# Linear attention ahead of a mixture of experts: state summed in PSUM, copied by ScalarE, state products in four quadrants, query decays made on the chip, gating work put off

## The chip, the core and the metric

The kernel runs on one core of a Trainium2 chip. A core has TensorE (PE: matrix products into PSUM; its weight loads are shown as PEld), VectorE (DVE), ScalarE (ACT), GpSimd (POOL), SyncE (SP, which here only issues transfers) and 16 DMA engines between HBM and the on-chip memory SBUF. Each engine works through its own list in order and waits on semaphores for the others. The metric is the device time of one execution in microseconds (us).

## What is computed

```python
state = zeros(B, H, D, D)                       # 4 batches, 8 heads, 64 x 64
for t in range(S):                              # 768 tokens of a batch
    state = gamma[h] * state + outer(k[:, :, t], v[:, :, t])
    y[:, :, t] = scale * (q[:, :, t] @ state)
x = y as (3072 tokens, 512)
logits = x @ w_gate                             # 8 experts, the largest takes the token
out = gate_w * sigmoid(x @ w_output_gate)[e] * (relu(x @ w1[e]) @ w2[e])
h = out @ w_in                                  # 512 x 2048
y = (h - tanh(h)) @ w_out                       # 2048 x 512
```

## The kernel before

The attention is computed in chunks of 128 tokens: 4 batches of 6 chunks make 24 tiles, n = 0 to 23, and c = n % 6 is the chunk within its batch. A chunk needs four products per head. *Scores*, k times q of the same chunk (L351), are masked and decayed by VectorE into `pt` (L344). The *state product* (L388) takes the 64 x 64 state `st` left by the earlier chunks of the batch and `qd`, the queries times a decay that depends on c (L362, GpSimd). The *masked product* (L392) takes v and `pt` and adds to the same bank, `o`. The *state update* (L405), kd times v with 128 tokens of depth, gives `up`; VectorE copies it to the next state (c = 0, L414) or adds it to the last one (L416). Chunk 0 of a batch has no state product, chunk 5 no update. All four are float32 products, which TensorE does in two passes, so eight heads make 16 instructions. Two heads form a pair hp and share a row of tiles: the head j = 0 of a pair lies on partitions 0 to 63, j = 1 on 64 to 127. Its features take the same half as its output half, so the state product of j = 0 uses the upper left quadrant of the array and that of j = 1 the lower right.

ScalarE copies `o` to `xT` (L410). TensorE turns it to token rows and computes the gate logits in one go (`tr`, L433); ScalarE copies the rows to `xr` (L436) and sends them to HBM (`xtok`, L441), VectorE sums the logits (`lp`, L440).

The loop over n (L596) writes this order into every engine's list: load of tile n + 3 (SP, four buffers `ld`), stores that are pending, from n = 5 on four loads `m` of a later weight (L207), expert weights at n = 15, 16, 17, then `attend(n)` (the last three products), `scores(n + 2)`, the work listed in `after` (ranks and slots of a finished group) and `rows(n)`. The decays of the queries are a table in HBM of 256 KB for each c from 1 to 5, loaded behind tiles 1 to 5 (L334).

The gating is done in groups of 12, 6 and 6 tiles. At a group's last tile come `onehot` (the chosen expert, L461 to L476), `values` (the table `ohv` of what is to be summed per slot, L484, L488), `chosen` (`z`, L499), and one tile later `ranks` (each token's place with its expert: small products `pre`, `rank`, and one mark `ohr` of 432 columns per tile, L516). `scale` (gate weights, from L540) fills the rest of `ohv`. `slots` multiplies marks and values into `ip` (L576) and adds them to `idxf` (L579), from which the index lists for the gathers come after the last tile (L684). The last group is cut at 3 and 5 tiles, and its last tiles are done behind the loop, which this text calls the tail.

VectorE's work that may wait stands in the lists `scales` and `convs`; `convs` splits the weight `m` in two parts by nine steps (VectorE's are L224 to L239, ScalarE's `keep` L221). `pump` issues what stands first in a list for ScalarE or GpSimd. At the end of each turn `fill([scales, convs], MOST)` issues VectorE's, up to a cost of MOST = 2.0; steps of `convs` are booked at 0.65, others at 0.2.

```python
def fill(lists, most):
    for ops in lists:
        while ops and ops[0][0] == "V" and most > 0:
            most -= ops[0][2] if len(ops[0]) > 2 else 0.2
            ops.pop(0)[1]()
```

Of the kernel before, what the change touches and what calls it, by code (L numbers as in the profile page):

```python
# [8 lines left out]
F32 = mybir.dt.float32  # L9
# [55 lines left out]
C_K = C_Q + (NCH - 1) * NPAIR * P  # L65
# [3 lines left out]
NCONA = C_W8 + E  # L69
# [5 lines left out]
NCONB = B_BIAS + 3  # L75


def const_tables():
# [7 lines left out]
    for c in range(1, NCH):  # L86
        for h in range(H):
            col = C_Q + ((c - 1) * NPAIR + h // 2) * P
            a[(h % 2) * D:(h % 2 + 1) * D, col:col + P] = SCALE * gam[h] ** (c * P + p)[None, :]
# [12 lines left out]
    return a.astype(np.float32), b.astype(np.float32)  # L102
# [7 lines left out]
def kernel(  # L110
# [179 lines left out]
    with ExitStack() as actx:  # L290
        psa = actx.enter_context(tc.tile_pool(name="psa", bufs=2, space=PSUM))
        banks.update(po=(psa, 2), pb=(psa, 2), pu=(psa, 1), pt=(psa, 3))
# [9 lines left out]
        st = [a1p.tile([P, NPAIR, D], F32, name=f"st{i}") for i in range(2)]  # L302
# [3 lines left out]

        loaded, pts, qds, kds, xts = {}, {}, {}, {}, {}

        def load(n):
            t = ap_.tile([P, 4, DM], F32, tag="ld", name=f"ld{n}", bufs=4)  # L310
            if n == 0:
# [4 lines left out]
                nc.sync.dma_start(ca[:, C_K:C_IOTA], cona[:, C_K:C_IOTA])  # L316
                nc.sync.dma_start(t[:, 2:4], qkv[n, :, 2:4])
# [8 lines left out]
            if n == 4:  # L326
                nc.sync.dma_start(ca[:, C_IOTA:], cona[:, C_IOTA:])
# [4 lines left out]
            if 1 <= n < NCH:  # L332
                col = C_Q + (n - 1) * DM
                nc.sync.dma_start(ca[:, col:col + DM], cona[:, col:col + DM])  # L334
            loaded[n] = t

        def scores(n):
# [20 lines left out]
            if c > 0:  # L358
                qd = ap_.tile([P, DM], F32, tag="qd", name=f"qd{n}", bufs=3)
                for half in (slice(0, DM // 2), slice(DM // 2, DM)):  # L360
                    col = C_Q + (c - 1) * DM + half.start
                    nc.gpsimd.tensor_tensor(  # L362
                        out=qd[:, half], in0=t[:, 0, half], in1=ca[:, col:col + DM // 2], op=ALU.mult
                    )
                qds[n] = qd
# [12 lines left out]
        def attend(n):  # L378
# [10 lines left out]
            for hp, j, r in heads:  # L389
                vs = hp * P + j * D  # L390
                ks = (j * NPAIR + hp) * P
                nc.tensor.matmul(  # L392
                    o[r, hp * P:(hp + 1) * P],
                    t[:, 3, vs:vs + D],
                    pt[:, ks:ks + P],
                    start=(c == 0 and hp == 0),
                    stop=(hp == NPAIR - 1),
                )
            qds.pop(n, None)
            if c < NCH - 1:  # L400
                up = bank("pu", f"up{n}")
                kd = kds.pop(n)
                for hp, j, r in heads:
                    head = slice(hp * P + j * D, hp * P + (j + 1) * D)
                    nc.tensor.matmul(  # L405
                        up[r, hp * D:(hp + 1) * D], kd[:, head], t[:, 3, head], start=(hp == 0),
                        stop=(hp == NPAIR - 1),
                    )
            xT = ap_.tile([P, DM], F32, tag="xT", name=f"xT{n}")
            nc.scalar.activation(xT, o, AF.Copy)  # L410
            if c < NCH - 1:
                new, old, add = st[(n + 1) % 2].rearrange("p a e -> p (a e)"), st[n % 2], up[:, 0:NPAIR * D]
# [178 lines left out]
        load(2)  # L591
        J0 = 2 * NFM - NPA
        convs, scales, soon, after = [], [], [], []
        nconv = 0
        firsts = [sum(GROUPS[:i]) for i in range(len(GROUPS))]
        for n in range(NT - 1):  # L596
# [15 lines left out]
            if n > 0:  # L612
                attend(n)
            pump(scales, False)
# [19 lines left out]
            if g + 1 in cuts[1:]:  # L634
# [3 lines left out]
                values(*a)  # L638
                chosen(*a)
# [12 lines left out]
            fill([scales, convs], MOST)  # L652
# [549 lines left out]
```

## Time and profile before

| | us |
|---|---|
| three runs | 1028.24, 1020.76, 1024.3 |
| median | 1024.3 |
| the profiled execution, its time | 1021.1 |
| its span in the trace | 1019.2 |

Times are microseconds unless marked ns. The profile is one execution; the span is what lies between its first and last instruction. A row of PE with x16 stands for the 16 passes of one product of a tile. In brackets behind a row of a timeline is the idle time of the engine just before it and what ended it. The profile's clock column gives the granted clock of TensorE as a share of full speed, and its DMA share is the mean busy share of the 16 DMA engines.

### The profile page before, as it was taken

How to read it: one execution, taken by the hardware profiler on the slowest of the kernel's cores; microseconds unless marked ns; L12 is line 12 of the kernel's file. 1: busy time of each engine (PE TensorE's matmuls, PEld its weight loads, DVE VectorE, ACT ScalarE, POOL GpSimd, SP SyncE). 2: the span in 40 equal slices, each digit the busy share in tenths (PEclk: the TensorE clock that was granted, in tenths of full speed). 3: DMA queues.
4: the chain of work that ended last, by engine and by line, in shares of the span. 5: the costliest groups of instructions: out<-in, count | busy, mean ns of one | idle time of the engine just before them, and what ended most of it. 6: DMA issues, size and time to landing. Idle time of an engine off the chain costs nothing.

```text
span 1019.2 us, 15927 instructions
## 1 busy us (share of the span) xinstructions
PE 984.2 (97%) x5754; PEld 844.1 (83%) x5754; DVE 789.6 (77%) x1193; ACT 575.5 (56%) x1008; POOL 429.7 (42%) x359
## 2 busy tenths in 40 slices
PE   8998979999999999999999999999999999999995
PEld 6887858899999999998888888888888888888884
DVE  3588867999999999944987777777777777777772
ACT  1332314545545455545876766677676667767662
POOL 4464514375575664642333343253334325333322
PEclk9999998999999999999999999999999999999998
DMA  8997633567476576764200010010001001000001
GB/s 317 368 333 269 250 117 121 167 224 229 155 250 194 185 234 191 250 194 169 73 21 11 32 32 21 1 52 22 11 32 32 22 1 51 12 1 22 21 1 44
DMA packets 43415, 120.54 MB, mean 118 GB/s; under 512 B 9410, under 2 KB 14274, under 8 KB 40514
## 3 DMA queue, kind: packets, MB, share of 16 engines
q1 hardware_dynamic: 34882, 99.78, 29.6%
q0 software_dynamic: 4992, 13.38, 4.1%
q10 hardware_dynamic: 3456, 6.29, 1.6%
q8 instruction: 47, 0.77, 0.3%
q14 instruction: 38, 0.31, 0.1%
HBM read 95.40 MB, written 24.03 MB: 117 GB/s over the span
## 4 chain that ended last, share of the span: by engine, by line
PE 90%; DVE 5%; DMA 3%; issue 1%; ACT 0%; POOL 0%; SPq 0%; POOLq 0%; DVEq 0%; ACTq 0%
PE mh L978 26%; PE ma L992 26%; PE ya L775 14%; PE ph L759 14%; PE sc L351 2%; PE o L392 2%; PE tr L433 2%; PE o L388 2%; DMA ld<-in_qkv 2%; PE xt L726 1%; DMA gx<-xtok,idx 1%; PE up L405 1%; DMA ca<-in_cona 1%; PE ip L576 0%; DVE gx L721 0%
## 5 line engine op out<-in xcount | busy, mean ns | idle before, releaser
L960 POOL TENSOR_TENSOR gl<-g,gh 128x512 fp32r<-128x512 f32 x96 | 124.2, 1294 | 346.8 <-ACT gh L959 344.3
L953 DVE COPY_PREDICATED g<-big,td 128x512 f32<-128x512 int32 x96 | 145.3, 1514 | 9.9
L978 PE MATMUL mh<-x2h,ml 128*128 128x512 f32 x384 | 152.7, 398 | 0.0
L978 PE MATMUL mh<-x2l,mh 128*128 128x512 f32 x384 | 152.3, 396 | 0.0
L978 PE MATMUL mh<-x2h,mh 128*128 128x512 f32 x384 | 151.9, 396 | 0.0
L992 PE MATMUL ma<-ml,gh 128*128 128x512 f32 x384 | 151.2, 394 | 0.0
L992 PE MATMUL ma<-mh,gh 128*128 128x512 f32 x384 | 151.0, 393 | 0.0
L992 PE MATMUL ma<-mh,gl 128*128 128x512 f32 x384 | 149.2, 389 | 0.0
L943 DVE SCALAR_TENSOR_TENSOR g<-s,mh 128x512 f32<-128x512 f32 x96 | 65.9, 687 | 101.7 <-ACT s L941 85.8
L186 ACT ACTIVATE wh<-wr 128x512 fp32r<-128x512 f32 x128 | 79.3, 628 | 108.9 <-PE ya L775 86.4
L939 ACT ACTIVATE u<-mh 128x512 f32<-128x512 f32 x96 | 57.5, 599 | 128.9 <-PE mh L978 125.5
L188 POOL TENSOR_TENSOR wl<-wr,wh 128x512 fp32r<-128x512 f32 x64 | 99.3, 1552 | 64.3 <-ACT wh L186 59.0
L759 PE MATMUL ph<-xh,wh 128*128 128x432 f32 x256 | 94.0, 367 | 0.1
L759 PE MATMUL ph<-xh,wl 128*128 128x432 f32 x256 | 93.0, 363 | 0.8 <-POOL wl L188 0.8
L775 PE MATMUL ya<-lo,wh 128*128 128x432 f32 x256 | 91.9, 359 | 0.2 <-DVE lo L763 0.2
L759 PE MATMUL ph<-xl,wh 128*128 128x432 f32 x256 | 91.5, 359 | 0.6 <-DVE xl L746 0.6
L775 PE MATMUL ya<-hi,wl 128*128 128x432 f32 x256 | 91.9, 359 | 0.0
L775 PE MATMUL ya<-hi,wh 128*128 128x432 f32 x256 | 91.5, 357 | 0.0
L978 PEld LDWEIGHTS mh<-x2h,ml 128*128 128x128 f32 x384 | 72.2, 188 | 17.6
L978 PEld LDWEIGHTS mh<-x2h,mh 128*128 128x128 f32 x384 | 72.4, 189 | 17.2
L992 PEld LDWEIGHTS ma<-mh,gh 128*128 128x128 f32 x384 | 72.0, 188 | 17.5
L978 PEld LDWEIGHTS mh<-x2l,mh 128*128 128x128 f32 x384 | 72.0, 188 | 17.1
(153 smaller groups left out, 2028.6 us busy)
## 6 DMA issues: line engine op xcount, KB each, us to landing
wr<-in_w SPq DMA_DIRECT2D x64, 512.0 KB
ld<-in_qkv SPq DMA_DIRECT2D x22, 1024.0 KB
m<-in_w SPq DMA_DIRECT2D x32, 512.0 KB
x2c<-y SPq DMA_DIRECT2D x32, 216.0 KB
xtok<-xr ACTq DMA_DIRECT2D x24, 256.0 KB
x2r<-x2c SPq DMA_DIRECT2D x24, 256.0 KB
dh<-keep SPq DMA_DIRECT2D x8, 256.0 KB
dl<-ta SPq DMA_DIRECT2D x8, 256.0 KB
```

The costliest lines, as they stand in the source:

```text
L186: nc.scalar.activation(hi, t[:, cs], AF.Copy)
L188: eng.tensor_tensor(out=lo, in0=t[:, cs], in1=f32(hi), op=ALU.subtract)
L351: nc.tensor.matmul(sc[g][:, cs], t[r, 1, cs], t[r, 0, cs], start=True, stop=True)
L388: nc.tensor.matmul(o[r, cs], st[n % 2][r, hp], qds[n][r, cs], start=(hp == 0), stop=False)
L759: nc.tensor.matmul(ph, a[:, cs], b[:, kk], start=(k == 0), stop=(k == 3 * KD - 1))
L775: nc.tensor.matmul(accs[e][dk], a[:, cs], b, start=(f == 0 and j == 0), stop=(f == NFE - 1 and j == 2))
L939: nc.scalar.activation(u, h, AF.Square)
L943: nc.vector.scalar_tensor_tensor(out=g, in0=s1, scalar=PB1, in1=h, op0=ALU.add, op1=ALU.mult)
L953: nc.vector.copy_predicated(g, big.bitcast(I32), td)
L960: nc.gpsimd.tensor_tensor(out=lo, in0=g, in1=f32(hi), op=ALU.subtract)
L978: nc.tensor.matmul(h, a[:, cs], c, start=(k == 0), stop=(k == 3 * KD - 1))
L992: nc.tensor.matmul(macc[b][t], a[:, cs], c[:, DM:2 * DM], start=(f == 0 and j == 0), stop=(f == NFM - 1 and j == 2))
```

## The change

- **State in PSUM.** The updates of a batch's five chunks add up in one PSUM bank `up`, cleared by the first product of chunk 0; ScalarE copies it to the one state tile `st` after each update. VectorE's copy and add are gone. The update is issued between the state products and the masked products.
- **Four quadrants.** The output `o` becomes one tile over two banks, one bank for each head j of a pair. The output half b of a head is j for the even pairs and the other half for the odd ones. So two pairs in a row use all four quadrants. Features come out in another order (`feature_order`), which the host's tables of the gate and of w1 follow.
- **Query decays.** Only the table for c = 1 is loaded. `decay(c)` makes the next ones from it, four ScalarE operations of 128 columns each, behind the loads of tile 2 and in the turns 0 to 2. A table of 12 columns (`C_W8` to the end) is loaded in tile 0's turn by itself.
- **Gating put off.** `values` and `chosen` go to the list `scales` at a cost of 0.8 and 0.3. The turn that holds `onehot` gives `fill` a budget smaller by `busy` = 0.25 times the root of the group's tiles + 1.

```diff
-            o = bank("po", f"o{n}")
+            o = psa.tile([P, 2, 512], F32, tag="po", name=f"o{n}", bufs=1)[:, :, 0:2 * P]
-            heads = [(hp, j, slice(j * D, (j + 1) * D)) for hp in range(NPAIR) for j in range(2)]
+            heads = [(hp, j, j ^ (hp & 1)) for hp in range(NPAIR) for j in range(2)]
+            def place(hp, j, b):
+                return o[half(b), j, hp // 2 * P:(hp // 2 + 1) * P]
             if c > 0:
-                for hp, j, r in heads:
-                    cs = slice(hp * P, (hp + 1) * P)
-                    nc.tensor.matmul(o[r, cs], st[n % 2][r, hp], qds[n][r, cs], start=(hp == 0), stop=False)
+                for hp, j, b in heads:
+                    nc.tensor.matmul(
+                        place(hp, j, b), st[half(j), hp], qds[n][half(j), hp * P:(hp + 1) * P], start=(hp < 2), stop=False
+                    )
+            if c < NCH - 1:
+                for hp, j, b in heads:
+                    head = slice(hp * P + j * D, hp * P + (j + 1) * D)
+                    nc.tensor.matmul(
+                        up[half(j), hp * D:(hp + 1) * D], kd[:, head], t[:, 3, head], start=(c == 0 and hp == 0),
+                        stop=(hp == NPAIR - 1), skip_group_check=True,
+                    )
+                nc.scalar.activation(st.rearrange("p a e -> p (a e)"), up, AF.Copy)
...
-            nc.scalar.activation(xT, o, AF.Copy)
-                if c == 0:
-                    nc.vector.tensor_copy(new, add)
-                else:
-                    nc.vector.tensor_tensor(out=new, in0=old.rearrange("p a e -> p (a e)"), in1=add, op=ALU.add)
+            nc.scalar.activation(xT.rearrange("p (j c) -> p j c", j=2), o, AF.Copy)
...
+        def decay(c):
+            for hp in range(NPAIR):
+                cs = slice(hp * P, (hp + 1) * P)
+                nc.scalar.activation(qt[c][:, cs], qt[c - 1][:, cs], AF.Copy, scale=ca[:, C_STEP + hp:C_STEP + hp + 1])
...
+                nc.sync.dma_start(ca[:, C_W8:], cona[:, C_W8:])
-            if 1 <= n < NCH:
-                col = C_Q + (n - 1) * DM
-                nc.sync.dma_start(ca[:, col:col + DM], cona[:, col:col + DM])
+            if n == 1:
+                nc.sync.dma_start(qt[1], cona[:, C_Q:C_Q + DM])
...
                 onehot(*a)
-                values(*a)
-                chosen(*a)
+                busy = 0.25 * (g + 1 - g0) ** 0.5 + 1.0
+                scales.append(("V", lambda a=a: values(*a), 0.8))
+                scales.append(("V", lambda a=a: chosen(*a), 0.3))
...
-            fill([scales, convs], MOST)
+            fill([scales, convs], MOST - busy)
+            busy = 0.0
```

On PE the products of tile 3 stand like this before; `tr` are the transposes of the tile before it, and x8 counts the eight heads.

```order
L433 MATMUL tr_0_385<-turn_rhs,xT_362 128x144 x2
L433 MATMUL tr_1_390<-turn_rhs,xT_362 128x144 x2
L388 MATMUL o_403<-qd_315,st_116 64x128 x8
L392 MATMUL o_403<-pt_302,ld_214 64x128 x8
L405 MATMUL up_420<-ld_214,kd_318 64x64 x8
```

And after the change (L412 is the state product, L419 the update, L427 the masked product):

```order
L449 MATMUL tr_0_400<-turn_rhs,xT_374 128x144 x2
L449 MATMUL tr_1_405<-turn_rhs,xT_374 128x144 x2
L412 MATMUL o_418<-qd_328,st 64x128 x8
L419 MATMUL up<-ld_222,kd_331 64x64 x8
L427 MATMUL o_418<-pt_315,ld_222 64x128 x8
```

The state update has moved ahead of the masked products; the number of products is the same.

On VectorE these rows follow the choice of experts for the first group (n = 11, `oh` is its table of chosen experts) before; `ta` and `va` are steps that split a weight, `pt` the masking of the scores of tile 13.

```order
L476 TENSOR_TENSOR oh_224<-ca,emax 128x96
L484 TENSOR_TENSOR ohv_225<-oh_224,ca 128x12x8
L488 TENSOR_SCALAR ohv_225<-oh_224,cb 128x12x8
L499 TENSOR_TENSOR z_222<-oh_224,lg_218 128x96
L540 TENSOR_REDUCE zs_228<-z_222 128x12
L541 TENSOR_SCALAR low_233<-zs_228 128x12
L224 TENSOR_SCALAR ta_938<-m_31_718 128x512
L227 SCALAR_TENSOR_TENSOR va_939<-m_31_718,ta_938 128x512
L233 TENSOR_SCALAR ta_938<-va_939 128x512
L414 COPY st_116<-up_999 128x256
L344 TENSOR_TENSOR pt_1035<-sc_0_1036,ca 128x512
```

After the change the same place reads:

```order
L492 TENSOR_TENSOR oh_235<-ca,emax 128x96
L500 TENSOR_TENSOR ohv_236<-oh_235,ca 128x12x8
L504 TENSOR_SCALAR ohv_236<-oh_235,cb 128x12x8
L364 TENSOR_TENSOR pt_1033<-sc_0_1034,ca 128x512
L364 TENSOR_TENSOR pt_1033<-sc_1_1035,ca 128x512
L528 TENSOR_TENSOR rt_237<-oh_235,pre_0_1052 128x96
L529 TENSOR_REDUCE rank<-rt_237 128x12
```

The selection `z`, the first rows of the scaling and the weight splitting have moved behind the next tile's masking, and the copy of the state is no longer in the list.

On VectorE's list in the tail, behind `oh` of the last group's second cut, these rows stand before (`rt` and `rank` are the ranks of tiles 21 and 22):

```order
L484 TENSOR_TENSOR ohv_1518<-oh_1517,ca 128x2x8
L488 TENSOR_SCALAR ohv_1518<-oh_1517,cb 128x2x8
L499 TENSOR_TENSOR z_1515<-oh_1517,lg_1511 128x16
L512 TENSOR_TENSOR rt_1519<-oh_1517,pre_3_1910 128x16
L513 TENSOR_REDUCE rank<-rt_1519 128x2
```

And after:

```order
L500 TENSOR_TENSOR ohv_1514<-oh_1513,ca 128x3x8
L504 TENSOR_SCALAR ohv_1514<-oh_1513,cb 128x3x8
L515 TENSOR_TENSOR z_1511<-oh_1513,lg_1507 128x24
L532 TENSOR_SCALAR ohr_1516<-iota,rank 128x432 x3
L500 TENSOR_TENSOR ohv_1514<-oh_1513,ca 128x2x8
L504 TENSOR_SCALAR ohv_1514<-oh_1513,cb 128x2x8
L515 TENSOR_TENSOR z_1511<-oh_1513,lg_1507 128x16
L528 TENSOR_TENSOR rt_1515<-oh_1513,pre_3_1882 128x16
L529 TENSOR_REDUCE rank<-rt_1515 128x2
```

Values, selection and the three marks of tiles 18 to 20 now stand in front of the ranks of tiles 21 and 22; on PE the 24 products `ip` of the marks of one group have moved with them, from ahead of tile 22's transposes to behind the last `pre`.

## Rows read from the trace of the kernel before

**Rows 1.** The page: busy time of each engine, share of the span, instructions.

```profile
PE 984.2 (97%) x5754; PEld 844.1 (83%) x5754; DVE 789.6 (77%) x1193; ACT 575.5 (56%) x1008; POOL 429.7 (42%) x359
```

**Rows 2.** Chain of waits, a steady tile: start us, us, what.

```profile
29.34 1.09 PE sc L351 x16
30.43 1.18 PE tr L433 x8
31.61 1.02 PE o L388 x16
32.63 1.02 PE o L392 x16
33.66 0.46 PE up L405 x16
```

**Rows 3.** Timeline of PE: start us, us, line, out<-in, [idle before, its releaser].

```profile
16.11 1.16 PE L351 MATMUL sc<-ld 64*128 64x128 f32 x16 [1.24 <-DMA ld<-in_qkv]
...
44.97 1.25 PE L433 MATMUL tr<-turn_rhs,xT 128*128 128x144 f32 x8 [1.69 <-ACT xT L410]
...
46.87 1.09 PE L388 MATMUL o<-qd,st 64*64 64x128 f32 x16 [0.65 <-DVE st L414]
...
65.72 1.16 PE L351 MATMUL sc<-ld 64*128 64x128 f32 x16 [1.83 <-DMA ld<-in_qkv]
...
80.17 1.97 PE L388 MATMUL o<-qd,st 64*64 64x128 f32 x16 [3.10 <-DVE st L414]
82.07 1.77 PE L392 MATMUL o<-pt,ld 128*64 128x128 f32 x16
...
117.74 1.09 PE L388 MATMUL o<-qd,st 64*64 64x128 f32 x16 [0.76 <-DVE st L416]
...
123.85 1.09 PE L388 MATMUL o<-qd,st 64*64 64x128 f32 x16 [1.26 <-DVE st L416]
```

**Rows 4.** Windows: us; busy PE, PEld, DVE, ACT, POOL; clock, DMA share, GB/s.

```profile
16.00:66.00 50.00, 45.68 (x684) 40.67 (x686) 29.75 (x63) 15.46 (x33) 26.44 (x39) 1.00 0.97 353
...
80.00:92.00 12.00, 11.83 (x158) 10.69 (x160) 10.66 (x42) 2.73 (x6) 5.43 (x9) 0.86 0.51 168
92.00:120.00 28.00, 26.87 (x419) 24.03 (x417) 21.09 (x65) 8.43 (x21) 11.58 (x17) 1.00 0.93 336
```

**Rows 5.** Timeline of the weight loads, one tile's masked products.

```profile
37.34 0.85 PEld L392 LDWEIGHTS o<-pt,ld 128*64 128x64 f32 x16 [0.17 <-issue]
```

**Rows 6.** Timelines of PE (scores of tile 0) and GpSimd (query decay of tile 20).

```profile
6.12 1.71 PE L351 MATMUL sc<-ld 64*128 64x128 f32 x16
...
108.00 1.43 POOL L362 TENSOR_TENSOR qd<-ld,ca 128x256 f32<-128x256 f32 x2 [3.66 <-DMA ld<-in_qkv]
```

**Rows 7.** By line, 0 to 142 us: busy, mean ns of one, idle before.

```profile
L436 ACT ACTIVATE xr<-tr 128x256 f32<-128x256 f32 x48 | 17.9, 382 | 36.3 <-PE tr L433 31.0 <-DMA xtok<-xr 1.9 <-PE tr L435 1.4
L410 ACT ACTIVATE xT<-o 128x512 f32<-128x512 f32 x24 | 14.3, 597 | 50.4 <-PE o L392 50.0 <-ACT xr L436 0.4
...
L416 DVE TENSOR_TENSOR st<-st,up 128x256 f32<-128x256 f32 x16 | 6.7, 416 | 7.7 <-PE up L405 7.6
```

**Rows 8.** Timeline of DVE around the first group's end.

```profile
77.84 0.98 DVE L227 SCALAR_TENSOR_TENSOR va<-m,ta 128x512 uint32<-128x512 uint32 x1
...
79.61 0.41 DVE L414 COPY st<-up 128x256 f32<-128x256 f32 x1
```

**Rows 9.** Timeline of SP: one transfer of few columns is issued.

```profile
2.75 0.43 SPq L316 DMA_DIRECT2D ca<-in_cona  x1
```

**Rows 10.** Timelines of DVE and PE in the tail.

```profile
127.28 0.18 DVE L484 TENSOR_TENSOR ohv<-oh,ca 128x24 bf16<-128x24 bf16 x1
127.60 0.81 DVE L516 TENSOR_SCALAR ohr<-iota,rank 128x432 bf16<-128x432 f16 x3
...
131.40 1.38 PE L576 MATMUL ip<-ohv,ohr 128*108 128x40 bf16 x24
...
137.69 0.17 DVE L462 TENSOR_REDUCE m<-lplast 128x1 f32<-128x8 f32 x1 [0.46 <-PE lplast L663]
```

More of the change, by code (lines that the diff above doesn't have):

```diff
@@ L68 @@
 C_W8 = C_TILE + NT
-NCONA = C_W8 + E
+C_STEP = C_W8 + E
+NCONA = C_STEP + NPAIR
 B_ID = 0
@@ L75, with feature_order @@
 NCONB = B_BIAS + 3
+def feature_order():
+    order = []
+    for j in range(2):
+        for k in range(NPAIR // 2):
+            for b in range(2):
+                hp = 2 * k + (b ^ j)
+                order += list(range((2 * hp + j) * D, (2 * hp + j + 1) * D))
+    return np.array(order)
 def const_tables():
@@ L85, in const_tables @@
         a[:, o:o + P] = np.where(dt >= 0, SCALE * gam[h] ** np.maximum(dt, 0), 0.0)
[L86 to L89, printed above, removed]
+    for h in range(H):
+        r, col = slice((h % 2) * D, (h % 2 + 1) * D), C_Q + (h // 2) * P
+        a[r, col:col + P] = SCALE * gam[h] ** (P + p)[None, :]
+        a[r, C_STEP + h // 2] = gam[h] ** P
     for c in range(NCH - 1):
@@ L301 @@
         turn_rhs = a1p.tile([P, KD, PG], F32, name="turn_rhs")
-        st = [a1p.tile([P, NPAIR, D], F32, name=f"st{i}") for i in range(2)]
+        st = a1p.tile([P, NPAIR, D], F32, name="st")
+        up = bank("pu", "up")[:, 0:NPAIR * D]
         maskt = ca[:, C_MASK:C_MASK + H * P]
@@ L305 @@
         w8 = ca[:, C_W8:C_W8 + E]
+        qt = {c: a1p.tile([P, DM], F32, name=f"qt{c}") for c in range(1, NCH)}
         loaded, pts, qds, kds, xts = {}, {}, {}, {}, {}
+        def decay(c):
+            for hp in range(NPAIR):
+                cs = slice(hp * P, (hp + 1) * P)
+                nc.scalar.activation(qt[c][:, cs], qt[c - 1][:, cs], AF.Copy, scale=ca[:, C_STEP + hp:C_STEP + hp + 1])
         def load(n):
@@ L381, in attend, with half @@
             pt = pts.pop(n)
[L382 to L389 removed]
+            o = psa.tile([P, 2, 512], F32, tag="po", name=f"o{n}", bufs=1)[:, :, 0:2 * P]
+            heads = [(hp, j, j ^ (hp & 1)) for hp in range(NPAIR) for j in range(2)]
+            def half(x):
+                return slice(x * D, (x + 1) * D)
+            def place(hp, j, b):
+                return o[half(b), j, hp // 2 * P:(hp // 2 + 1) * P]
+            if c > 0:
+                for hp, j, b in heads:
[3 more added lines that the diff above has]
+            if c < NCH - 1:
+                kd = kds.pop(n)
+                for hp, j, b in heads:
[5 more added lines that the diff above has]
+                nc.scalar.activation(st.rearrange("p a e -> p (a e)"), up, AF.Copy)
+            for hp, j, b in heads:
                 vs = hp * P + j * D
@@ L392, in attend @@
                 nc.tensor.matmul(
[L393 to L397, printed above, removed]
+                    place(hp, j, b), t[:, 3, vs:vs + D], pt[:, ks:ks + P], start=(c == 0 and hp < 2), stop=(hp >= 2)
                 )
             qds.pop(n, None)
[L400 to L408, printed above, removed]
-            xT = ap_.tile([P, DM], F32, tag="xT", name=f"xT{n}")
-            nc.scalar.activation(xT, o, AF.Copy)
-            if c < NCH - 1:
-                new, old, add = st[(n + 1) % 2].rearrange("p a e -> p (a e)"), st[n % 2], up[:, 0:NPAIR * D]
-                if c == 0:
-                    nc.vector.tensor_copy(new, add)
-                else:
-                    nc.vector.tensor_tensor(out=new, in0=old.rearrange("p a e -> p (a e)"), in1=add, op=ALU.add)
+            xT = ap_.tile([P, DM], F32, tag="xT", name=f"xT{n}")
+            nc.scalar.activation(xT.rearrange("p (j c) -> p j c", j=2), o, AF.Copy)
             xts[n] = xT
@@ L591 @@
         load(2)
+        decay(2)
         J0 = 2 * NFM - NPA
         convs, scales, soon, after = [], [], [], []
-        nconv = 0
+        nconv, busy = 0, 0.0
         firsts = [sum(GROUPS[:i]) for i in range(len(GROUPS))]
```

18 lines of the change are left out of this document (9 added, 9 removed).

## The prediction

> **What bounds the kernel now.** I read the busy shares first. TensorE (PE) is busy 97% of the 1019.2 us span, ahead of VectorE (DVE, 77%) and ScalarE (ACT, 56%) [rows 1]; the reader sees that only PE's own time and PE's waits can matter. The change touches the attention loop alone, so I then followed the chain of waits through the first 142 us. A steady tile there is nothing but PE: scores 1.09, transposes 1.18, state products 1.02, masked products 1.02, state update 0.46, together 4.77 us [rows 2]. What breaks the row stands in PE's timeline; its larger waits from 16 us on are four for the state `st` that DVE makes, one for `xT` that ACT copies and two for a load [rows 3]. After the loop the expert stages keep PE busy to the end, so what the loop gains or loses I pass on one to one. The windows show the second limit: from 16 to 66 us the DMA engines are 97% busy, and 93% from 92 to 120 [rows 4]. PE cannot run ahead of its loads there.
>
> **The change, part by part.**
>
> *State products four side by side.* L388 steps 1.02 us for 16 passes, two per head. The two heads of a pair sit on one diagonal of the array, so two passes run at a time: eight steps. 0.17 us of it is the idle time when PE's weight loads meet a new shape [rows 5], leaving 0.85, or 0.106 a step. After, two head pairs take the two diagonals, and four steps remain: 0.43. I take 0.42 us saved per tile, in 20 tiles. That two passes with different rows do overlap is seen in the scores: issued eight of one row half and then eight of the other, tile 0 took 1.71 us; alternating, 1.16 [rows 3, 6]. Four at once is not seen here; lower bound 0, upper 0.43. The Trainium skill, "TensorE: Matmul & The Clock Gate", Part 3 (Packing small matmuls), has four row tiles at 3.07 times, not 4; by it four steps would take 0.85 × 2 / 3.07 = 0.55, an estimate, the saving would be 0.30 a tile and the sum 1.1 us smaller (nine tiles of the later stages). The order of halves in the masked products also becomes 0,1,1,0, so passes in one column half come four in a row, not two. Bounds: nothing, and the 0.55 us (1.71 − 1.16) that eight in a row cost. I take nothing, as the overlap in tile 0 began with several passes still to go.
>
> *State in PSUM, copied by ACT.* DVE loses 16 adds of 416 ns [rows 7] and 4 copies of 0.41 us [rows 8], 8.3 us. The waits on them go: 0.65 at 46.87, 3.10 at 80.17, 0.76 at 117.74, 1.26 at 123.85 [rows 3]. The 3.10 came about because `st` stood behind gating and weight splitting on DVE: the state update was done early, yet `st` was copied only at 79.61, after `va` at 77.84 (0.98 us) [rows 8]. PE idled and then ran slowly: L388 took 1.97 and L392 1.77 instead of 1.09 each (1.09 is the same row's length at 117.74) [rows 3], the granted clock having a mean of 0.86 of full (2.4 GHz) from 80 to 92 us, so part of it at 1.2 GHz [rows 4]. With the wait goes that 0.88 + 0.68 = 1.56. In return ACT gets 20 copies. It does not have the row in the trace; the bounds are 382 ns (`xr`, 256 columns) and 597 ns (`xT`, 512) [rows 7], and I take 0.38, the same size. Per tile ACT then does 0.38 + 0.60 + 2 × 0.38 = 1.74 of some 4.35 us. The copy is issued ahead of `xT`, and its reader is a whole tile later, behind scores and transposes (2.27 us [rows 2]), so it is covered; `xT` waits for it at most 0.38 beyond the masked products, and its reader, the transposes, stands behind 1.09 us of scores. What could be late next is this copy behind `keep` of the weight splitting, which on ACT waits for a transfer: that is the 1.69 at 44.97 [rows 3]. That transfer queues with the loads and comes forward with them, and PE comes forward too; I count half of the wait as gone, 0.8. "TensorEngine Tiling (Array Packing)" of the Trainium skill, PSUM Bottleneck, advises ScalarE and VectorE both for emptying PSUM; the change does the contrary. The rows agree with the change here: ACT is the emptier engine, 56 against 77%.
>
> *Query decays on chip.* Four transfers of 256 KB go, 1.05 MB, at 353 GB/s [rows 4] 3.0 us of DMA time, all before tile 6. 16 ACT operations of 128 columns come (bounds 0 and 0.38 each); the first four run while PE waits for the load of tile 2, for which it waits up to 16.11 [rows 3], later ones in ACT's idle time. If that cover went, 4 × 0.38 = 1.5 a tile would sit before `xT`. One small transfer is new; its issue takes SP 0.43 [rows 9]. Taken 0.2 of it, as the first loads queue behind it.
>
> *Gating put off.* By the order rows, values and selection of a group leave the place right behind `onehot` and are let in by a budget. For the first group that moves the work behind `st`, which is counted above. At the end it costs: DVE meets three `ohr` marks (0.81), values and `z` of group two (three of 0.18, as at 127.28) in front of the last groups' ranks: +1.4, less the 0.46 that it idles at 137.69 [rows 10]. And 24 index products of group two, 1.38 us on PE at 131.40 [rows 10], move behind the last ranks, where PE otherwise waits for DVE. That makes +2.3. Bounds: +1.2 if PE's part is hidden, +4 if the adds on DVE and two pieces of splitting come on top.
>
> *The sum,* by stage.
> - To the scores of tile 12 (65.72): nine tiles × 0.42 = 3.8, + 0.65 + 0.8 + the 1.83 DMA wait = 7.1 if loads allowed. But they allow 3.0 from the removed decays and 50 × 0.03 = 1.5 of idle DMA time, less 0.2: **−4.3**.
> - To the scores of tile 15: two tiles, 0.84 + 3.10 + 1.56 = **−5.5**. The loads have landed by then, since PE stood still.
> - To the scores of tile 23: seven tiles, 2.9 + 0.76 + 1.26 = 4.9. DMA has 12 × 0.49 + 28 × 0.07 = 7.8 us of idle time to take up, but its loads had little slack: `qd` of tile 20 had waited 3.66 for its load when it began at 108.00 [rows 6]. I leave 1.4 as new waits (between 0 and twice that): **−3.5**.
> - Tail: **+2.3**; the last two tiles' 0.84 vanish, DVE being late there.
>
> Together −11.0. The profiled execution took 1021.1, so 1010.1 on its base; it lies 3.2 below the median of the runs (1024.3). The four known times have a mean of 1023.6; I set the sum against that: **1012.6**.
>
> **Rivals.**
> 1. *Four never run at once.* L388 stays at 1.02. Then 3.3 in the first stage, 4.7, 2.0 and +2.3 remain: −7.7, **1015.9**. For: no row shows four. Against: rows and columns each overlap by themselves.
> 2. *DMA takes the gain.* Loads wait for buffers as before, idle DMA time is not taken up: only the removed decays help the first stage (3.0 − 0.2 = 2.8), and of the idle 12 × 0.49 = 5.9 us from 80 to 92 the second stage's 5.5 use all but 0.4 for the third: 2.8 + 5.5 + 0.4 − 2.3 = 6.4, **1017.2**. For: the load rows above. Against: buffers come free earlier when PE does.
> 3. *What is put off piles up.* If four more splitting operations (0.98 as `va`) stand before the last ranks, the tail costs 6.2: −7.1, **1016.5**. For: the budget only shortens what is let in. Against: DVE has 8.3 us less.
> 4. *Changing the diagonal drains PE* (the other side). The products now change diagonal three times a tile. Were each to cost the 0.17 that a new shape costs [rows 5], 60 × 0.17 = 10.2, and the 0.42 gains are gone too: −7.7 + 10.2 = +2.5, **1026.1**. It decides from 7.7 / 60 = 0.13 us a change. Against: the idle time stands only where the shape changes. The Trainium skill, "TensorEngine Tiling (Array Packing)", Key Properties, says the same: a new tiling mode drains, a new tile does not.
>
> **How the numbers follow.** Chances: forecast 0.55, rival 1 0.12, rival 2 0.16, rival 3 0.12, rival 4 0.05. A measurement of this kernel can tell about 1%, 10.2 us, from no change. The forecast's own bounds: no new DMA waits at 20–23 and a tail of +1.2 give −13.5, with the first stage free of DMA (7.1) −16.3; a tail of +4, −9.3. From 1023.6 that is 1007.3 to 1014.3, with a base 1 us to either side 1006 to 1015, which holds about the forecast's 0.55; up to 1019 rivals 1 to 3 come in. Range **1006 to 1019**. Faster by over 1%: 0.55 × 0.75, and a fifth of rivals 1 to 3, 0.49. Slower by over 1%: 0.03, half of rival 4. Within 1%: 0.48.
>
> **What would show it.** L412 near 0.60 us in the chain, 1.02 under rival 1. No PE wait on `st` after onehot of the first group, and no drop of the granted clock around 80 us. First wait of PE on a load: if the scores of tile 12 come 4 us earlier than 65.72 the DMA account is right; at 2.8 or less, rival 2. From the last scores to the first gathered rows: 2 us longer, or 6. The prediction is wrong if ACT's copy shows up as a releaser of PE in most tiles, or if the weight loads of L412 show idle time inside a tile.

## The result and the profile after

Ten runs of each kernel gave a median of 1017.2 us after the change (1014.5 to 1021.2) and 1026.4 before (1020.8 to 1028.9); the ratio is 0.9915, interval 0.9899 to 0.9932. On a second occasion, beside three of the variants below, the ratio was 0.9952 (0.9934 to 0.9970). So the change saves 5 to 9 us, less than the 11.0 of the sum. Both intervals lie below 1, so the sign was right; the size is known only to within these two. The four variants that each take back one part of the change, and the one with the splitting two turns later, were timed on other occasions without the change beside them, so their ratios can be set against it only to within this spread.

The page of the changed kernel has the same bound as before:

```profile
PE 981.3 (97%) x5754; PEld 837.9 (82%) x5754; DVE 784.4 (77%) x1173; ACT 587.2 (58%) x1044; POOL 428.2 (42%) x359
```

A steady tile in the chain of waits after (start us, us, what; L412 is the state product, L419 the update, L427 the masked product):

```profile
22.86 1.18 PE tr L449 x8
24.04 0.60 PE o L412 x16
24.64 0.62 PE up L419 x16
25.25 0.88 PE o L427 x16
26.13 1.09 PE sc L371 x16
```

1.09 + 1.18 + 0.60 + 0.62 + 0.88 is 4.37 us, 0.40 less than the 4.77 of [rows 2]. The state product fell by 0.42. The 0.17 us of a new shape [rows 5] now lies in front of the update (0.62 for 0.46), and the masked products gave it up (0.88 for 1.02). The weight loads of the same tile show it:

```profile
23.97 0.42 PEld L412 LDWEIGHTS o<-qd,st 64*64 64x64 f32 x16
24.57 0.55 PEld L419 LDWEIGHTS up<-ld,kd 128*64 128x64 f32 x16 [0.17 <-POOL qd L381]
```

PE's timeline after, the places that answer to [rows 3] and one new one:

```profile
12.04 1.27 PE L419 MATMUL up<-ld,kd 128*64 128x64 f32 x16 [3.53 <-POOL kd L387]
...
18.52 1.16 PE L371 MATMUL sc<-ld 64*128 64x128 f32 x16
...
46.86 1.88 PE L449 MATMUL tr<-turn_rhs,xT 128*128 128x144 f32 x8 [3.07 <-ACT xT L432]
48.66 1.13 PE L412 MATMUL o<-qd,st 64*64 64x128 f32 x16
...
66.84 1.24 PE L371 MATMUL sc<-ld 64*128 64x128 f32 x16 [2.04 <-DMA ld<-in_qkv]
68.01 2.29 PE L449 MATMUL tr<-turn_rhs,xT 128*128 128x144 f32 x8
```

All waits for `st` are gone, in this trace as in the second. But PE waits 3.53 us at 12 us, where before its masked products waited 1.77 for their load; the wait for `xT` has grown from 1.69 to 3.07; and the scores of tile 12 begin at 66.84, not at 65.72 less 4.3. Behind each of the three waits the same products take about twice as long (`tr` 2.29 against 1.25 elsewhere). The windows say why (columns as in [rows 4]):

```profile
8.00:20.00 12.00, 8.47 (x91) 7.50 (x91) 4.57 (x16) 4.08 (x12) 5.89 (x10) 0.72 1.01 385
16.00:66.00 50.00, 45.60 (x701) 39.09 (x700) 28.48 (x59) 23.80 (x59) 29.03 (x41) 0.96 0.93 321
66.00:80.00 14.00, 12.75 (x169) 10.84 (x171) 9.64 (x21) 4.96 (x11) 7.51 (x11) 0.88 0.93 337
80.00:92.00 12.00, 12.00 (x198) 10.47 (x199) 11.62 (x39) 4.96 (x13) 7.00 (x11) 1.00 0.94 323
92.00:120.00 28.00, 27.23 (x452) 23.59 (x452) 25.06 (x72) 12.09 (x29) 15.87 (x23) 1.00 0.84 321
```

The granted clock, 1.00 or 0.50 (2.4 or 1.2 GHz) at any one time, is 0.72 on average from 8 to 20 us and 0.88 from 66 to 80, where the kernel before lost it from 80 to 92 (0.86, [rows 4]). From 80 to 120 PE is busy almost without a break. DMA, idle for half of 80 to 92 before, is now 94% busy there.

This table sets the stages side by side. Its times are the starts of the first score product of tiles 12, 15 and 23 and of the first expert product (`ph`), from PE's timeline of each kernel, in us; the second execution of each is told of below.

| kernel | to tile 12 | 12 to 15 | 15 to 23 | 23 to `ph` | `ph` to end | span |
|---|---|---|---|---|---|---|
| before | 65.7 | 18.5 | 42.1 | 29.0 | 863.9 | 1019.2 |
| before, second execution | 66.6 | 22.1 | 42.5 | 28.8 | 865.4 | 1025.4 |
| after | 66.8 | 14.5 | 37.1 | 32.3 | 865.3 | 1016.0 |
| after, second execution | 69.3 | 15.7 | 37.2 | 31.4 | 865.8 | 1019.4 |
| masked first in tile 0 | 66.1 | 14.7 | 38.1 | 33.6 | 865.8 | 1018.4 |
| small table later | 68.6 | 13.0 | 36.9 | 32.5 | 866.6 | 1017.6 |
| splitting two turns later | 60.9 | 14.2 | 37.8 | 38.8 | 865.9 | 1017.7 |
| weight loaded a turn earlier | 63.6 | 13.0 | 36.9 | 32.9 | 865.7 | 1012.1 |
| three repairs | 65.1 | 13.0 | 37.7 | 33.6 | 865.3 | 1014.6 |
| pairs, not quadrants | 68.8 | 13.8 | 39.9 | 32.0 | 866.7 | 1021.3 |
| decays from HBM | 65.6 | 14.5 | 38.1 | 32.9 | 865.3 | 1016.4 |
| gating at once | 66.2 | 15.4 | 39.4 | 30.2 | 865.4 | 1016.7 |
| state copied by VectorE | 65.2 | 13.8 | 38.4 | 32.3 | 866.4 | 1016.0 |
| quadrants almost alone | 66.4 | 18.2 | 40.1 | 31.2 | 864.3 | 1020.2 |

### The profile page after: what moved, and what is told of

It is laid out like the page before. It is cut to its first block, busy times and chain, and to the rows that moved or that the text cites. A ratio compares the mean times of both kernels' runs of the same rounds, so it can differ in the third digit from the quotient of the medians.

```text
span 1016.0 us, 15930 instructions
## 1 busy us (share of the span) xinstructions
PE 981.3 (97%) x5754; PEld 837.9 (82%) x5754; DVE 784.4 (77%) x1173; ACT 587.2 (58%) x1044; POOL 428.2 (42%) x359
## 4 chain that ended last, share of the span: by engine, by line
PE 89%; DVE 4%; DMA 4%; issue 1%; ACT 0%; POOL 0%; SPq 0%; ACTq 0%; POOLq 0%; DVEq 0%
PE mh L999 27%; PE ma L1013 26%; PE ph L780 14%; PE ya L796 14%; PE tr L449 2%; PE sc L371 2%; DMA ld<-in_qkv 2%; PE o L427 1%; PE o L412 1%; PE xt L747 1%; PE up L419 1%; DMA m<-in_w 1%; DMA gx<-xtok,idx 1%; DVE wl L200 1%; PE ip L592 1%
```

## The experiments

The theory after the first trace: the quadrants and the freed state bring what was summed, from tile 12 on; ahead of tile 12 the gain is lost because PE now waits at the start for `kd`, and because ScalarE, which now carries the state, stands before `keep` of the weight splitting. Each wait is followed by a stretch at half clock. The rivals: DMA bounds that stretch anyway; or the gain is not from where it was thought to be. Where only one run was made, its stages can be read; its total tells little.

**The kernel before, again** (no edit).

> The kernel before once more, unchanged, for a second profile. Theory A (the profiled execution of before was a lucky one): its first trace took 1021.1, 5 us under the median of ten runs, 1026.4; a second trace shows PE waits or slow-clock stretches in the first 145 us that the first trace did not have, with the scores of tile 23 later than 126.4. Theory B (scatter is spread over the whole execution): the scores of tile 23 stand within 1 us of 126.4, and the last product is late by what the span is longer.

One run took 1027.3 us, a span of 1025.4. PE's timeline:

```profile
66.63 2.08 PE L351 MATMUL sc<-ld 64*128 64x128 f32 x16 [2.67 <-DMA ld<-in_qkv]
...
84.07 1.97 PE L388 MATMUL o<-qd,st 64*64 64x128 f32 x16 [3.09 <-DVE st L414]
```

The wait for the load was 2.67 instead of 1.83, and this time the scores after it ran at half clock (2.08 for 1.16 us). The scores of tile 23 began at 131.2 instead of 126.4. Theory A holds: of the 6.2 us between the two spans, 4.6 lie ahead of `ph`. One trace was a poor base; these two differ mainly in how long PE ran at half clock behind its waits.

**The change, again** (no edit).

> The changed kernel unchanged, on the chip of the next three, for their comparison. Its time against the kernel before is expected at 0.990 to 0.994; the trace should again show the wait of PE for kd at 12 us, for xT behind ScalarE's keep at 44 to 48 us and half-clock stretches behind both. If one of the two is missing at the same total, that wait was not part of the price.

1020.0 us median, ratio 0.9952 (0.9934 to 0.9970).

```profile
47.89 2.25 PE L449 MATMUL tr<-turn_rhs,xT 128*128 128x144 f32 x8 [2.79 <-ACT xT L432]
...
69.31 2.08 PE L371 MATMUL sc<-ld 64*128 64x128 f32 x16 [3.45 <-DMA ld<-in_qkv]
```

Both new waits are there again, with longer slow products. Expected was 0.990 to 0.994; it came out just worse.

**Start: masked products first in tile 0.**

```diff
+            if n > 0:
+                update()
...
+            if n == 0:
+                update()
```

> The changed kernel, with the masked products of tile 0 ahead of its state update, as before the change; all other tiles as changed. In the changed kernel PE waited 3.53 us for kd of tile 0 and then ran at half clock to about 18 us; the scores of tile 2 began at 18.5, against 16.1 before. Theory A (the order is to blame: the update needs kd, which GpSimd makes only after the load, 0.6 us; PE's idle stretch then costs the clock): the masked products begin about 1 us earlier, PE's wait falls below 3 us, the half-clock stretch goes, scores of tile 2 at 16 to 17. Theory B (the load itself is late, because a new small transfer stands ahead of it): the wait goes down by 0.6 at most, the clock falls all the same, scores of tile 2 at 17.5 or later.

One run, 1020.1 us.

```profile
10.23 1.98 PE L431 MATMUL o<-pt,ld 128*64 128x128 f32 x16 [1.75 <-DMA ld<-in_qkv]
...
17.20 1.16 PE L371 MATMUL sc<-ld 64*128 64x128 f32 x16 [1.27 <-DMA ld<-in_qkv]
```

The wait fell to 1.75 and tile 2 came 1.3 us earlier, so the order has its part (A); the clock fell all the same (the 1.98). Of the 1.3 us, 0.7 were left at tile 12 and nothing at tile 23 (118.9 against 118.5).

**Start: the small table behind the query decays.**

```diff
-                nc.sync.dma_start(ca[:, C_W8:], cona[:, C_W8:])
                 nc.sync.dma_start(t[:, 2:4], qkv[n, :, 2:4])
...
                 nc.sync.dma_start(qt[1], cona[:, C_Q:C_Q + DM])
+                nc.sync.dma_start(ca[:, C_W8:], cona[:, C_W8:])
```

> The changed kernel, with the new table of 12 columns loaded behind the first query decays (in tile 1's turn) instead of ahead of the keys and values of tile 0. Theory B (the transfer in front makes the load late: it landed about 1.8 us later than before): kd of tile 0 can begin at 9.6 to 10.2 instead of 11.4, PE's wait falls to about 2 us, the clock holds, scores of tile 2 at 16 to 17. Theory A (order): kd begins 0.5 earlier, the wait is still about 3 us and the clock falls.

One run, 1019.4 us.

```profile
11.31 1.02 PE L419 MATMUL up<-ld,kd 128*64 128x64 f32 x16 [2.95 <-POOL kd L387]
```

Tile 2 began at 18.6. Theory B has little for it: the wait is still 2.95, `kd` begins 0.7 us earlier only (10.65 for 11.38). Nor is the load always late: in the next run, whose start is that of the changed kernel, PE began the same update at 9.22, without a fall of the clock. When the keys and values of tile 0 land differs from execution to execution by over 2 us in equal code; why stays open. A cost of the table of about 1 us is not ruled out: `kd` began at a median of 10.5 us in the eight traces with the table in front, 9.4 in the six without.

**ScalarE: the splitting two turns later.**

```diff
-                convs += piece(J0 + nconv, cva_p)
+                late.append((max(n, NCH + 1), piece(J0 + nconv, cva_p)))
...
+            while late and late[0][0] <= n:
+                convs += late.pop(0)[1]
```

> The changed kernel, with the first step of the weight splitting (ScalarE's keep, which waits for a 512 KB transfer) written two turns later; the transfer itself is issued where it was. In the changed kernel ScalarE stood 4.9 us before keep at 44.3, the copies of the state and of the output behind it, PE waited 3.07 at 46.9 and then ran at half clock to about 51. Theory A (ScalarE, now the carrier of the state, is blocked by keep): wait and slow stretch go, scores of tile 9 about 46.5 instead of 51.7; of these 5 us the DMA takes back some at tiles 11 and 12, so 1 to 4 us of the total remain, 1013 to 1016. Theory B (DMA is the bound there): a wait for the load of tile 9 to 11 takes its place, scores of tile 12 stay at 66 to 67, total unchanged.

1022.0 us, ratio 0.9957 (0.9936 to 0.9978). The wait for `xT` at 46.9 is gone; tile 9 began at 45.3 instead of 51.7 and tile 12 at 60.9 instead of 66.8, of which 2.6 were there at tile 2 already. So what held PE up there was ScalarE standing before `keep`, not the loads of the tiles, and theory B falls. For comparison, ScalarE's timeline of the changed kernel at that place:

```profile
44.33 0.66 ACT L233 ACTIVATE keep<-m 128x512 f32<-128x512 f32 x1 [4.94 <-DMA m<-in_w]
...
45.94 0.38 ACT L423 ACTIVATE st<-up 128x256 f32<-128x256 f32 x1 [0.40 <-ACT xr L452]
46.22 0.59 ACT L432 ACTIVATE xT<-o 128x512 f32<-128x512 f32 x1
```

`keep` waits 4.94 us for its transfer, and rows, state and output stand behind it. Yet the total did not gain, against theory A's 1013 to 1016. From tile 23 to `ph` this run took 38.8 us, 6.5 more than the changed kernel: the last weight's splitting now falls into the tail (timelines of VectorE, ScalarE and PE of this run):

```profile
124.93 0.69 DVE L258 SCALAR_TENSOR_TENSOR va<-keep,va 128x512 f32<-128x512 f32 x1
...
125.66 0.63 ACT L265 ACTIVATE keep<-va 128x512 fp32r<-128x512 f32 x1 [4.26 <-DVE va L258]
...
126.83 1.07 PE L686 MATMUL lplast<-wgs,xT 128*128 128x16 f32 x8 [3.46 <-ACT xT L432]
```

That is the pile-up of rival 3, made by the repair and not by the change.

**ScalarE: the transfer one turn earlier**, the splitting steps in the turns where they were.

```diff
-            if n >= NCH - 1 and nconv < NPA and len(m64) < 2:
+            convs += late
+            late = []
+            if n >= NCH - 2 and nconv < NPA and len(m64) < 2:
                 load_m(J0 + nconv, cva_p)
-                convs += piece(J0 + nconv, cva_p)
+                late += piece(J0 + nconv, cva_p)
```

> The changed kernel, with the 512 KB transfer for each weight to be split issued one turn earlier, and its splitting steps in the turns where they are (in the run with the steps two turns later the loop gained 5.5 us, but the last weight's splitting fell into the tail and took it back). Theory A (ScalarE is blocked by keep, and the loop's gain reaches the end if nothing falls into the tail): PE's wait at 44 to 48 goes, scores of tile 23 at 113 to 115.5 instead of 118.5, no wait of PE of 3 us before the last products, total 2 to 5 us below the changed kernel. Theory B (the transfer in front now delays the loads of tiles 8 and 9): a load wait of 1.5 us or more at 42 to 46 takes its place, scores of tile 23 at 117 or later, total within 1.5 us of the changed kernel.

1016.2 us, ratio 0.9922 (0.9894 to 0.9949), where the change had 0.9952 on the same chip: 3.8 us of medians. The two intervals overlap.

```profile
42.17 1.16 PE L371 MATMUL sc<-ld 64*128 64x128 f32 x16 [1.60 <-DMA ld<-in_qkv]
...
52.64 1.16 PE L371 MATMUL sc<-ld 64*128 64x128 f32 x16 [1.53 <-DMA ld<-in_qkv]
...
63.63 1.16 PE L371 MATMUL sc<-ld 64*128 64x128 f32 x16 [2.21 <-DMA ld<-in_qkv]
```

The wait for `xT` is gone, scores of tile 23 at 113.5, and the tail (32.9) holds. Against the first trace of the change the gain is 5.0 us at tile 23 and 3.9 in the span, as theory A had it; 1.9 of it was there at tile 2 already (16.60 for 18.52), where the code is the same. But 5.3 us of load waits have come in the place; theory B's mechanism is real, and takes part of it. Whether the kernel before would have gained as much from the earlier transfer was not tried.

**The three repairs together** (the edits of the first, second and fourth variant).

> The changed kernel with three repairs: the weight transfer one turn earlier, tile 0's masked products ahead of its update, the small table behind the query decays. Theory A (the losses of the start are made good too, scores of tile 2 at 16 to 17): total 1 to 2 us below the run with the early transfer alone, 3 to 6 below the changed kernel. Theory B (what the start gains is taken back by load waits up to tile 12, as in the run with the order alone, where 1.3 us at tile 2 were 0.7 at tile 12): total equal to the run with the early transfer alone within 1.5 us.

1016.5 us, ratio 0.9912 (0.9890 to 0.9934). It is the lowest ratio of all variants, with no difference to the early transfer alone that could be measured: theory B. Its interval ends where that of the change on the same chip begins; the twelve times of the two runs with the early transfer have a median of 1016.5, the eleven of the change 1020.0. So the earlier transfer is worth some 3.5 us. The start is good in this trace, with a clock of 1.00 from 8 to 20 us (as it was with the splitting later, whose start is unmended):

```profile
8.00:20.00 12.00, 8.08 (x125) 7.07 (x126) 4.92 (x17) 4.34 (x14) 7.18 (x12) 1.00 1.02 405
```

But loads took it back (2.04 at 42.8, 2.69 at 65.1).

**The quadrants undone.**

```diff
-            heads = [(hp, j, j ^ (hp & 1)) for hp in range(NPAIR) for j in range(2)]
+            heads = [(hp, j, j) for hp in range(NPAIR) for j in range(2)]
-                return o[half(b), j, hp // 2 * P:(hp // 2 + 1) * P]
+                return o[half(j), hp * P:(hp + 1) * P]
```

(with one bank for `o`, two buffers, and the features in their own order)

> The changed kernel with the four quadrants undone: each head's output half is its own half again, one bank for o, two buffers; the state in PSUM, ScalarE's copy, the early update, the decays and the gating stay as changed. Theory A (the quadrants are worth 0.42 a tile, and PE's gain comes through): L412 steps 1.02 instead of 0.60 in 20 tiles, the total is 4 to 8 us longer than that of the changed kernel, 1021 to 1025, less than 8.4 because DMA waits in the first 66 us are filled by it. Theory B (DMA hides it): L412 is 1.02, and the total moves by under 3 us.

1020.3 us, ratio 0.9955 (0.9932 to 0.9978). In the chain the state product is

```profile
26.96 1.02 PE o L407 x16
```

and the stage from tile 15 to 23 takes 39.9 us instead of 37.1: 2.8, where 7 × 0.42 is 2.9. There the gain comes through, to within the 1 us by which this stage differs between traces that leave it alone (36.9 to 38.1). As a whole the ratio is that of the second measurement of the change and 0.40% above the first; the runs don't settle what of the 8.4 us reaches the total. The span was 5.3 longer, of which 2.0 arose ahead of tile 12.

**The decays from HBM again.**

```diff
-            if n == 1:
-                nc.sync.dma_start(qt[1], cona[:, C_Q:C_Q + DM])
+            if 1 <= n < NCH:
+                nc.sync.dma_start(qt[n], cona[:, C_Q + (n - 1) * DM:C_Q + n * DM])
```

(and no `decay`, no small table by itself)

> The changed kernel with the query decays loaded from HBM again (four more transfers of 256 KB, no new small table, no ScalarE decays); all else as changed. Theory A (the removed transfers bring 3 us of DMA time in the first 66 us, the new small table costs 2 at the start): the start is as before the change (scores of tile 2 at 16 to 17), the load waits up to tile 12 grow by 3 to 5 us, total 1 to 4 us longer than the changed kernel. Theory B (the transfers are hidden anyway): the total is 1 to 3 us shorter, by the mended start.

1019.6 us, ratio 0.9942 (0.9920 to 0.9964). To tile 12 it took 65.6 us, less than the change, with 1.05 MB more to load. Inconclusive on the 3.0 us: the start was better by 1.6, and this variant takes more SBUF and starts its gathers late:

```profile
139.62 1.20 POOL L728 DMA_INDIRECT gx<-xtok,idx  x1 [19.27 <-DVE sslot L707]
```

The index list stood at 134.9 there. What can be said: no loss from the four transfers shows.

**The gating at once.**

```diff
-                busy = 0.25 * (g + 1 - g0) ** 0.5 + 1.0
-                scales.append(("V", lambda a=a: values(*a), 0.8))
-                scales.append(("V", lambda a=a: chosen(*a), 0.3))
+                values(*a)
+                chosen(*a)
```

> The changed kernel with the gating done at once again (values and selection right behind the choice of experts, full budget for the turn). Theory A (once the state is copied by ScalarE, nothing on PE waits for DVE at the group's end, and putting off only costs the tail 2.3 us): PE shows no wait of over 1 us around 76 to 82 us, the products of group two are back ahead of tile 22's transposes, the index list is ready 2 us sooner relative to the scores of tile 23, total 1 to 3 us shorter. Theory B (the put-off is what keeps PE fed): a wait of PE of 1 to 3 us for the masked scores comes at 76 to 82, with a fall of the clock, total 1 to 4 us longer.

1019.3 us, ratio 0.9941 (0.9916 to 0.9967).

```profile
81.65 1.75 PE L371 MATMUL sc<-ld 64*128 64x128 f32 x16 [0.78 <-DVE pt L364]
...
127.03 1.38 PE L592 MATMUL ip<-ohv,ohr 128*108 128x40 bf16 x24
```

The products of group two are back in the loop and the tail is 2.1 us shorter (30.2 for 32.3); from tile 15 to 23 it is 2.3 longer, with scores waiting for the masking behind the gating. Theory A has the tail, theory B the masked scores, though its wait is 0.78 instead of 1 to 3 us and the clock stays at 1.00. In the total no difference shows.

**The state copied by VectorE.**

```diff
-                nc.scalar.activation(st.rearrange("p a e -> p (a e)"), up, AF.Copy)
+                nc.vector.tensor_copy(st.rearrange("p a e -> p (a e)"), up)
```

> The changed kernel with the copy of the summed state done by VectorE instead of ScalarE; the sum stays in PSUM, all else as changed. Theory A (the gain came from taking the state off VectorE): PE waits for st come back at 46, 80, 112 to 124, 3 to 6 us in all, total 2 to 6 us longer than the changed kernel. Theory B (with the gating put off VectorE is early enough, and ScalarE is the one that is blocked, by keep): no wait for st over 0.8 us, the wait at 46.9 is smaller, total the same or up to 2 us shorter.

1018.7 us, ratio 0.9931 (0.9910 to 0.9951), between the two of the change.

```profile
44.49 1.34 PE L449 MATMUL tr<-turn_rhs,xT 128*128 128x144 f32 x8 [2.52 <-ACT xT L432]
46.39 1.13 PE L412 MATMUL o<-qd,st 64*64 64x128 f32 x16 [0.55 <-DVE st L423]
...
81.95 0.67 PE L412 MATMUL o<-qd,st 64*64 64x128 f32 x16 [0.66 <-DVE st L423]
```

Two waits for `st`, of 0.55 and 0.66; theory B. With the gating put off, no difference shows between the two copiers. And the wait for `xT` is still 2.52, where the change had 3.07 and 2.79: ScalarE stands before `keep` whether it carries the state or not.

**The quadrants almost alone:** decays from HBM, gating at once, VectorE's copy, the update behind the masked products; that is the three edits before with the order of the products undone.

> The four quadrants almost alone: as in the kernel before, the decays come from HBM, the gating is done at once, the state is written by VectorE and the update stands behind the masked products; from the change stay the quadrants with their two-bank output and the sum in PSUM (so VectorE copies instead of adding). Theory A (the waits for st come back and are not less than before): L412 at 0.60, waits of PE for st at 46, 77 to 81 (about 3 us, with a fall of the clock) and 110 to 125, scores of tile 23 at 121 to 124, total 2 to 6 us below the kernel before and 3 to 6 above the changed one. Theory B (the quadrants are the whole gain): total within 1.5 us of the changed kernel.

1022.0 us, ratio 0.9968 (0.9948 to 0.9988).

```profile
81.96 0.67 PE L411 MATMUL o<-qd,st 64*64 64x128 f32 x16 [3.10 <-DVE st L423]
...
116.68 0.67 PE L411 MATMUL o<-qd,st 64*64 64x128 f32 x16 [0.93 <-DVE st L423]
...
122.61 0.67 PE L411 MATMUL o<-qd,st 64*64 64x128 f32 x16 [1.51 <-DVE st L423]
```

VectorE's timeline has the copy at 81.40, behind the splitting:

```profile
80.65 0.83 DVE L245 TENSOR_SCALAR ta<-va 128x512 uint32<-128x512 uint32 x1
81.40 0.41 DVE L423 COPY st<-up 128x256 f32<-128x256 f32 x1
```

The three larger waits of [rows 3] behind `st` are back, even though L411 takes 0.60 (the fourth, 0.65, is 0.43 at 46.81). That is theory A's mechanism, if not its size: the total is 3.3 us below the kernel before, but only 2.0 above the change on the same chip, whose interval it overlaps. VectorE's copy or the gating at once, each alone (the two runs before), did not bring the wait of 3.10. Here both stand together, with the old decays and order; that the two suffice without these is not shown.

## Why the prediction came out as it did

The first measurement, 1017.2 us, lay within the range; the second, 1020.0, just above it. The first is 4.6 above the forecast: 2.8 of it is the base (1026.4 where 1023.6 was taken), 1.8 the change, which saved 9.2 where the sum had 11.0; at the second it saved 5.3. That the first time lay within the range was in part luck: rivals 1 to 3, at 1015.9, 1017.2 and 1016.5, are all nearer to it than the forecast, and the second largest term of the sum did not come. The stages of the table add up to −3.2 us between the two first traces and to −6.0 between the two second ones. So the mechanisms are told from the stages, and what each is worth in the total stays open: every run that takes back one part lies at 0.9931 to 0.9955, inside or beside the change's own 0.9915 to 0.9952, and the sum in PSUM was never undone by itself.

- **Four quadrants:** right. 0.60 in the chain, 0.42 less, a measured 0.40 a tile with the shifted 0.17. Rival 1 falls. The four steps took 0.43. The 3.07 times of the Trainium skill ("TensorE: Matmul & The Clock Gate", Part 3), from which 0.55 was estimated, is not what this product shows. Rival 4 falls too: in each of the 20 tiles L412's weight loads run through without idle time between them, though they change diagonal three times; only in two half-clock stretches (48.66 and 70.22) 0.28 us stands in front of them. The trace agrees with the Trainium skill, "TensorEngine Tiling (Array Packing)", Key Properties.
- **Waits for `st`:** right; none is left. The one at 80 us, the largest, did not come back with VectorE's copy or with the gating at once alone. ScalarE's copy took 0.38, as taken, and PE waits for it in neither trace of the change.
- **To tile 12:** wrong. −4.3 was put down; measured +1.1 and +2.7. By the prediction's own sign (2.8 or less) this would be rival 2, but the DMA engines were less busy than before (0.93 for 0.97 from 16 to 66). Two terms failed.

The update ahead of the masked products was costed at nothing in tile 0, where its `kd` is the last to be ready: tile 2 came 2.4 us late (18.52 for 16.11), 3.2 in the second execution. Not all of this is the order. Over all traces, tile 2 began at 15.9 to 19.5 in the nine with the update first (median 17.8), and at 16.1 to 17.2 in the five with the masked products first (median 16.4); the clock from 8 to 20 us was under 1.00 in eight of the nine and one of the five. The rest goes largely with when the load landed (`kd` at 8.56 us and tile 2 at 15.91 with the splitting later, 11.38 and 18.52 in the first trace of the change).

And of the wait for `xT`, half was counted as gone, though the text named `keep` as what could be late next; it grew by 1.4 and 1.2. The transfer for `keep` was to come forward with PE. It was issued in step with PE, but then took longer (timelines of SP and ScalarE, before; of SP after, whose `keep` at 44.33 is shown above):

```profile
34.59 0.43 SPq L207 DMA_DIRECT2D m<-in_w  x1
42.70 0.68 ACT L221 ACTIVATE keep<-m 128x512 f32<-128x512 f32 x1 [3.62 <-DMA m<-in_w]
```

```profile
35.32 0.71 SPq L219 DMA_DIRECT2D m<-in_w  x1
```

From issue to `keep` it is 9.0 us after the change and 8.5 in its second execution, 8.1 and 8.0 before; why stays open. PE stood ready 0.2 and 0.4 sooner after the issue. From `keep` to the transposes it is 2.53 instead of 2.27, so the state's copy, which the first theory blamed, adds only 0.26 of the 1.4 and 1.2. Behind the wait four products took 1.6 us more, 4.87 in the chain for 3.28, part of it at half clock. The trace with the splitting later reached tile 12 at 60.9, 4.8 ahead of before, so the −4.3 was to be had where ScalarE is not blocked.

- **Tile 12 to 15:** −5.5 was put down, −4.0 and −6.4 came. The first lost its part to a half-clock stretch at 68 us, behind the load wait; in the second pair both kernels had one there.
- **Tile 15 to 23:** −5.0 and −5.3 against −3.5. The 1.4 of new load waits did not come; idle DMA time was taken up (0.51 to 0.94 from 80 to 92). Rival 2 falls here; ahead of tile 12 it is what the repairs ran into.
- **Tail:** +2.3 was put down, +3.3 and +2.6 came, of which 2.5 and 2.1 lie ahead of the first gather, the rest behind it. VectorE's part is as expected:

```profile
128.19 0.81 DVE L532 TENSOR_SCALAR ohr<-iota,rank 128x432 bf16<-128x432 f16 x3
...
130.26 0.16 DVE L478 TENSOR_REDUCE m<-lplast 128x1 f32<-128x8 f32 x1
```

The three marks stand there, and the idle time ahead of `m` [rows 10] is gone. The products of group two went with it:

```profile
131.30 2.07 PE ip L592 x36
```

36 products in one piece, 24 of them new. The run with the gating at once gave 2.1 us back, 1.4 of it ahead of the first gather. The first gather starts 15.56 us behind the scores of tile 23 before, 18.08 after:

```profile
141.92 1.20 POOL L711 DMA_INDIRECT gx<-xtok,idx  x1 [15.15 <-DVE ex L550]
```

```profile
136.54 1.20 POOL L732 DMA_INDIRECT gx<-xtok,idx  x1 [15.93 <-DVE ex L564]
```

Rival 3 did not happen in the change.

- **Base:** the sum was set against a mean of four times. Two executions of before differ by 6.2 us in span, so a sum from one trace was good to no better than that. Even from `ph` to the end, which the change leaves alone, the traces differ by 2.8 us (863.9 to 866.7).

## What to carry to other kernels

The share of busy time of an engine says nothing on how long it stands in its queue: look for the longest wait of any instruction on it, and ask what stands behind. Here that was `keep`, and what PE missed behind it was `xT`, which ScalarE copied before the change too. The transfer that `keep` waited for did not keep pace with a faster PE (9.0 us for 8.1). In a loop that takes waits in turn, removing one is worth only what the next one leaves; the gain has to be followed to the point where the next stage begins. A step moved forward must be costed in the first turn by itself, where its inputs are the last to arrive.

## What the runs showed of the hardware that was not expected

- Four 64 × 64 float32 products at once take half the time of two at once: 16 passes in 0.60 us instead of 1.02, which is 0.43 instead of 0.85 without the 0.17 of a new shape; no idle time when the diagonal changes.
- Waits of PE of like length were followed by half the granted clock or not. Of PE's 32 waits of 2.0 us or more between 5 and 130 us in the fourteen traces, 27 had a stretch with a granted clock under 1.00 soon behind them (after the change `tr` took 2.29 for 1.25). Five had not, among them 2.69 us at 65.06 with the three repairs and the longest, 3.22 us, in the run with the decays from HBM:

```profile
46.70 1.25 PE L448 MATMUL tr<-turn_rhs,xT 128*128 128x144 f32 x8 [3.22 <-ACT xT L431]
```

- One shorter wait, 1.75 us at 10.23 with the masked products first, was followed by half clock all the same.
- The keys and values of tile 0 were ready for `kd` between 8.6 and 11.4 us in kernels whose code is equal up to there.
